# Where a scheduler puts scores, norms and key preparations in a top-k attention with two MoE layers, and which engine makes the low parts

## Chip, cores and metric

The kernel runs on one core of one Trainium2 chip. The metric is device time in microseconds, the median of several executions. The engines are TensorE (PE in the rows; PEld is its weight load), VectorE (DVE), ScalarE (ACT), GpSimd (POOL) and SyncE (SP), whose queue issues the DMAs. Each engine works through its instructions in order.

## The reference

For 4 batches, 8 heads, 576 positions and head dimension 64, attention keeps the 32 largest scores of each row, then two MoE layers follow on the 2304 x 512 result.

```python
scores = scale * np.matmul(q, k.transpose(0, 1, 3, 2))
kth = np.partition(scores, -top_k, axis=-1)[..., -top_k:-top_k + 1]
scores = np.where(scores >= kth, scores, -1000000000.0)
attn = np.exp(scores - np.max(scores, axis=-1, keepdims=True))
attn = attn / (np.sum(attn, axis=-1, keepdims=True) + 1e-09)
x = attn @ v                                        # -> (2304, 512)
x = ((1 / (1 + np.exp(-(x @ w_gate)))) * (x @ w_val)) @ w_out
h = np.maximum(x @ w_in, 0.0)
out = (h * h) @ w_out2
```

## The kernel before

**Chunks and blocks.** The 2304 rows are 18 row tiles of 128, and these form 11 chunks: tiles 0, 1, 2, 3 singly (chunks 0 to 3), then 4 and 5 (chunk 4), 6 and 7 (chunk 5), 8 and 9 (chunk 6) and so on to 16 and 17 (chunk 10). Attention works on pairs of heads of a chunk; a *block* is one row tile with one head, 144 in all, 8 in a small chunk and 16 in a large one. A name such as `S_11_0` in an order is tile 11, head 0; `x_6` belongs to chunk 6.

**A block.** `queries` (line 307) transposes a tile's queries on TensorE and splits them into a high part that ScalarE casts (L319) and a low part that DVE subtracts (L320). `scores` (L344) multiplies with the split keys into the one PSUM tile `sp`, and ScalarE copies the result to a tile `S` (L347; four buffers). `softmax` searches the 32 largest on DVE: four times `max` (L358) and three times `match_replace` (L364) into a working tile `W` (three buffers). Then GpSimd prepares thresholds (L372, L373, L380), ScalarE cuts and exponentiates (L376, L386, L387), GpSimd makes the low part of the weights inside `S` (L391, L394), and a transposing DMA on SP's queue (L410) brings them to `PT`. `values16` (L482) multiplies them with the values, ScalarE copies (L503) and GpSimd scales into the chunk's `xt` (L504).

**After a chunk.** `split_x` splits the finished x in two f16 parts: squares on ScalarE (L685), column norms with a matrix of ones on TensorE (L688), a reduce and a scale on DVE (L690), then the split itself. Then the chunk's MoE layers run, almost all of their time on TensorE (L738, L778, L841, L862).

**Keys and values.** `prep_keys` loads a batch's keys for a pair of heads, transposes them on TensorE, lets ScalarE cast the high part (L171) and DVE subtract the low part (L172), and stores both in DRAM, from which later blocks load them (`kst`, three buffers, L299). It is called one pair ahead of the first use. `prep_values` loads and squares values; `split_values` splits them and stores them (`vm` holds a buffer of `S`, `vom` one of `W`).

**What sets the order.** The attention is a generator, the MoE another; the main loop emits them interleaved, attention ahead of the MoE of the chunk before. A scheduler then orders each engine's instructions by its own model of time and by priorities. `add_manual_dep(..., NOSYNC)` is a dependence for this scheduler alone: it makes an instruction stand after another one in the scheduler's time and places no semaphore. In the generator, `head(n + 1)` emits the next block's scores, `tail` the values of an earlier block, and `late` is called by `softmax` when the searches are emitted:

```python
            with tc.high_priority(offset=int(up[0])):
                head(n + 1)
                if n > 0 and units[n - 1][0].ci < TCI:
                    tail(n - 1)
                if pr.ci >= TCI - 2:

                    def late(mark, n=n):
                        while late_values:
                            split_values(*late_values.pop(0), mark)
                        if units[n - 2][0].ci >= TCI:
                            tail(n - 2, mark)
```

## Time and profile before

| | before |
|---|---|
| median of 3 runs | 1325.46 us (1323.99 to 1329.02) |
| the profiled execution, its own time | 1327.31 us |
| span of its trace | 1325.5 us |
| mean granted clock of TensorE | 0.942 |
| busy: TensorE, DVE | 1190.7 us (90%), 999.0 us (75%) |
| busy: ScalarE, GpSimd | 807.8 us (61%), 809.7 us (61%) |
| largest groups on DVE | the searches, L358 and L364 |
| DMA | 157.95 MB, mean 119 GB/s |

The share of an engine is an average over stages that differ: the first 200 us convert weights, the middle runs searches next to MoE matmuls, the last 190 us are MoE alone. A matmul's end is modelled, so a busy TensorE is not TensorE at its peak. What a step is worth has to be read in its own stage.

### The profile page before, as it was taken

Reading aid. Unit: us, or ns where it says so; the run is one execution under the profiler, and the core shown is the slowest. Engines: PE = TensorE matmul, PEld = TensorE weight load, DVE = VectorE, ACT = ScalarE, POOL = GpSimd, SP = SyncE. Lnnn points to the kernel's source line nnn. Section 1 sums busy time; section 2 is a strip of 40 time slices with the busy share of each in tenths; the row PEclk is TensorE's granted clock in tenths of the full one; section 3 lists DMA queues with packets and bytes.
Section 4 is the critical chain, followed back from the end, with each engine's and each line's share of the span. In section 5 each row is a group of like instructions: output and inputs, shape, how many; then the busy total and the mean of one; then the engine's idle time right before and its main releaser. Section 6 shows DMA issues by size and latency. Waiting matters only on the chain.

```text
span 1325.5 us, 30239 instructions
## 1 busy us (share of the span) xinstructions
PE 1190.7 (90%) x11357; PEld 947.1 (71%) x11357; DVE 999.0 (75%) x2040; ACT 807.8 (61%) x1584; POOL 809.7 (61%) x1324
## 2 busy tenths in 40 slices
PE   6756999977989879889986999999999999999998
PEld 5544886865868758756874768877886887787775
DVE  6999996897899989887989777878999899210010
ACT  4777786776666676656666665656677657323122
POOL 1798868867566576557556764575657647424223
PEclk9658999979999979979996999999999999999999
DMA  7988851233356454656745255556444333100000
GB/s 196 330 285 293 269 178 28 77 100 101 102 120 144 115 129 98 147 115 155 179 109 128 72 128 136 123 124 152 100 100 108 97 82 65 44 1 1 17 1 16
DMA packets 263409, 157.95 MB, mean 119 GB/s; under 512 B 213344, under 2 KB 229728, under 8 KB 263264
## 3 DMA queue, kind: packets, MB, share of 16 engines
q1 hardware_dynamic: 263264, 156.03, 45.4%
q8 instruction: 89, 1.46, 0.5%
q14 instruction: 56, 0.46, 0.1%
HBM read 103.55 MB, written 19.40 MB: 93 GB/s over the span
## 4 chain that ended last, share of the span: by engine, by line
PE 54%; POOL 11%; DVE 10%; DMA 8%; ACT 8%; issue 6%; SPq 2%; ACTq 0%; POOLq 0%; DVEq 0%
PE ph L841 12%; PE acc L862 11%; PE pg L738 7%; PE pv L738 6%; PE acc L778 6%; PE sp L344 5%; DMA PT<-S 3%; DVE mx L358 3%; DVE W L364 3%; PE xp L482 3%; POOL S L391 2%; ACT W L387 1%; DMA kst<-ks 1%; ACT W L376 1%; ACT S L386 1%
## 5 line engine op out<-in xcount | busy, mean ns | idle before, releaser
L358 DVE MAX8 mx<-W 128x8 f32<-128x576 f32 x432 | 327.5, 758 | 10.5
L841 PE MATMUL ph<-x,wi_w 128*128 128x256 f16 (+1 forms) x1920 | 207.6, 262 | 7.1 <-ACT x L817 6.3
L364 DVE MATCH_REPLACE8 W<-mx,W 128x576 f32<-128x576 f32 x288 | 213.7, 742 | 0.0
L391 POOL TENSOR_TENSOR S<-W,S 128x512 f16<-128x512 f32 x112 | 130.0, 1160 | 128.7 <-ACT W L387 127.6
L862 PE MATMUL acc<-w_w,rh 128*128 128x512 f16 x816 | 194.8, 380 | 4.0 <-POOL rh L854 4.0
L841 PEld LDWEIGHTS <-wi_w 128*128 128x128 f16 x1920 | 167.9, 100 | 41.5 <-issue 9.9
L376 ACT ACTIVATE W<-S,bs 128x576 f32<-128x576 f32 x144 | 111.6, 775 | 106.7 <-POOL bs L372 106.2
L344 PE MATMUL sp<-kst,qt 128*128 128x288 f32 x608 | 139.2, 337 | 25.7 <-ACT S L347 14.5
L738 PE MATMUL pg<-xs,wg_w 128*128 128x256 f16 (+1 forms) x1440 | 157.7, 261 | 2.8 <-POOL xs L702 2.0
L738 PE MATMUL pv<-xs,wv_w 128*128 128x256 f16 (+1 forms) x1440 | 153.1, 258 | 1.2 <-ACT th L748 0.6
L738 PEld LDWEIGHTS <-wg_w 128*128 128x128 f16 x1440 | 124.6, 99 | 21.4 <-issue 3.7
L862 PEld LDWEIGHTS <-rh 128*128 128x128 f16 x816 | 77.1, 98 | 82.6 <-POOL rh L854 5.9
L347 ACT COPY S<-sp 128x576 f32<-128x576 f32 x144 | 91.6, 636 | 72.9 <-DMA PT<-S 36.3
L778 PEld LDWEIGHTS <-wo_w 128*128 128x128 f16 x1440 | 123.0, 99 | 17.9 <-issue 5.1
L738 PEld LDWEIGHTS <-wv_w 128*128 128x128 f16 x1440 | 123.1, 99 | 16.7 <-issue 3.4
L778 PE MATMUL acc<-gh,wo_w 128*128 128x256 f16 (+1 forms) x1200 | 123.4, 255 | 4.6 <-POOL gh L754 2.8
L344 PEld LDWEIGHTS sp<-kst,qt 128*128 128x128 f32 x608 | 93.6, 196 | 43.7 <-ACT S L347 20.0
L750 DVE TENSOR_TENSOR th<-pv,th 128x512 f32<-128x512 f32 (+1 forms) x60 | 36.2, 604 | 111.4 <-PE pv L738 105.1
L853 POOL TENSOR_TENSOR r<-r 128x512 f32<-128x512 f32 (+1 forms) x80 | 74.5, 932 | 72.7 <-ACT rh L852 66.3
L358 DVE MAX8 mx<-S 128x8 f32<-128x576 f32 x144 | 107.0, 743 | 9.4 <-ACT S L347 9.4
L364 DVE MATCH_REPLACE8 W<-mx,S 128x576 f32<-128x576 f32 x144 | 106.9, 742 | 0.0
L386 ACT ACTIVATE S<-W,bs 128x576 f16<-128x576 f32 x112 | 86.7, 775 | 19.5 <-POOL bs L380 15.7
(336 smaller groups left out, 2172.1 us busy)
## 6 DMA issues: line engine op xcount, KB each, us to landing
kst<-ks SPq DMA_DIRECT2D x104, 288.0 KB, 3.1
v<-vd SPq DMA_DIRECT2D x40, 320.0 KB, 3.2
qn<-in_q_dram SPq DMA_DIRECT2D x128, 64.0 KB, 2.3
wi_r<-in_moe_w_in_dram SPq DMA_DIRECT2D x16, 512.0 KB, 6.6
w_r<-in_moe_w_out_dram SPq DMA_DIRECT2D x16, 512.0 KB, 4.9
wg_r<-in_moe_w_gate_dram SPq DMA_DIRECT2D x12, 512.0 KB, 6.5
wv_r<-in_moe_w_val_dram SPq DMA_DIRECT2D x12, 512.0 KB, 6.9
wo_r<-in_moe_w_out_dram SPq DMA_DIRECT2D x12, 512.0 KB, 6.0
```

What stands on the lines that cost most here:

```text
L344: nc.tensor.matmul(sp[:, e, 0:HALF], l, r, start=(x == 0), stop=(x == len(ops) - 1))
L347: nc.scalar.copy(ss.rearrange("p (e s) -> p e s", e=2), sp[:, :, 0:HALF])
L358: m8 = nc.vector.max(mx[:, r], cur)
L364: nc.vector.match_replace(wk, mx[:, r], cur, NEG)
L376: nc.scalar.activation(wk, ss, AF.Prelu, bias=bs[:, 0:1], scale=1.0, alpha=BIG)
L386: nc.scalar.activation(pp[:, 0:S], wk, AF.Exp, bias=bs[:, 1:2], scale=SCALE)
L391: nc.gpsimd.tensor_tensor(pp[:, S + ST : 2 * S], wk[:, 0:SM], pp[:, 0:SM], op=ALU.subtract)
L738: nc.tensor.matmul(pp[:, e * N : (e + 1) * N], wblk(wd, a, c, f0, P), xs[:, b_, c, :], start=(e == 0 and n == 0), stop=(n == 3 * KM - 1), ...
L778: nc.tensor.matmul(acc[:, d // 2, (d % 2) * N : (d % 2 + 1) * N], wblk("wo", a, f, d * P, P), gh[:, b_, e * N : (e + 1) * N], start=(f == ...
L841: nc.tensor.matmul(ph[:, e * N : (e + 1) * N], wblk("wi", a, c, f0, P), x2[:, b_, c, :], start=(e == 0 and n == 0), stop=(n == 3 * KM - 1) ...
L853: nc.gpsimd.tensor_tensor(r, r, r, op=ALU.mult)
L862: nc.tensor.matmul(acc2[:, i, 0:DM], gh[:, b_, e * N + i * P : e * N + (i + 1) * P], wblk("w2", a, f, 0, DM), start=(f == 0 and x == 0), s ...
```

## The change

1. *Scores.* From chunk 4 on, `head(n + 1)` is called out of `late`, and each score matmul has an order dependence on the first `max` of the block before (`marks[0]`).
2. *Column norms of x.* From chunk 4 on, `square_x` lets ScalarE square x where x is finished; the norm matmuls come in the `late` of the next block, behind its last `max` (`marks[3]`).
3. *Late keys.* Batches 2 and 3 are prepared in the same pairs as the values of these batches, a chunk earlier than before. Loads go out at one block (`slots`), the rest (`finish_keys`) two blocks later behind the last `max`. The tail part of the keys lies in tag `we`, the high part in a buffer of `W` instead of `kst`. ScalarE copies the whole transposed keys over the loaded ones, and GpSimd subtracts instead of DVE. The values' tail part moves to tag `we` as well.
4. *Queries.* For all chunks: ScalarE copies the whole transposed queries over the loaded ones, and GpSimd subtracts the low part instead of DVE.

```diff
@@ prep_keys / finish_keys
+        tag, bufs = ("we", 3) if late else ("qn", 2)
+        ke = apool.tile([ST, 2, D], F32, tag=tag, bufs=bufs, name=f"ke_{b}_{hp}")
...
+        if late:
+            return kn, kv, ke
+        finish_keys(b, hp, kn, kv, ke, keep)
+
+    def finish_keys(b, hp, kn, kv, ke, keep=False, after=None):
+        tag, bufs = ("kst", KST) if after is None else ("W", 3)
+        kh = apool.tile([P, S], F32R, tag=tag, bufs=bufs, name=f"kp_{b}_{hp}")
...
+                if after is not None:
+                    tc.add_manual_dep(mm.ins, after.name, NOSYNC, reason="loaded by then")
...
+            else:
+                whole = kl.bitcast(F32)[:, c0 : c0 + w]
+                nc.scalar.copy(whole, pt[:, 0:w])
+                nc.gpsimd.tensor_tensor(
+                    kl[:, c0 : c0 + w], whole, kh[:, c0 : c0 + w], op=ALU.subtract
+                )
@@ queries
-                    nc.vector.tensor_tensor(
-                        qt[:, 1, :, sl], p3[:, :, sl], qt[:, 0, :, sl], op=ALU.subtract
+                    whole = qn.rearrange("p j a d -> p j (a d)")[:, :, sl]
+                    nc.scalar.copy(whole, p3[:, :, sl])
+                    nc.gpsimd.tensor_tensor(
+                        qt[:, 1, :, sl], whole, qt[:, 0, :, sl], op=ALU.subtract
                     )
@@ scores
+                    if after is not None:
+                        tc.add_manual_dep(mm.ins, after.name, NOSYNC, reason="free by then")
@@ attention
+            if n in slots:
+                late_k.append((*slots[n], *prep_keys(*slots[n], late=True)))
...
+                    if (b, pr.hp) not in done:
+                        done.add((b, pr.hp))
+                        slots[n + 1] = (b, pr.hp)
...
+                    elif after is not None:
+                        square_x(pr.ci, pr.xt)
+                        late_x.append(pr)
...
+                def late(marks, n=n, pr=pr):
+                    if pr.ci >= SCI:
+                        head(n + 1, marks[0])
+                        if units[n - 1][0].ci < TCI:
+                            tail(n - 1)
+                    todo_k = late_k[:]
+                    del late_k[:]
+                    while late_values:
+                        split_values(*late_values.pop(0), marks[3])
+                    while late_x:
+                        p = late_x.pop(0)
+                        xsp[p.ci] = split_x(p.ci, p.xt, marks[3])
+                    if units[n - 2][0].ci >= TCI:
+                        tail(n - 2, marks[3])
+                    for b, hp, kn, kv, ke in keys_due:
+                        finish_keys(b, hp, kn, kv, ke, after=marks[3])
+                    keys_due[:] = todo_k
```

How this moves instructions shows at three places. The first is TensorE's order where chunk 6 ends (`sp_11_0`, `sp_11_1`: scores of the next chunk's tile 11; `xp_9_3`: values of the last pair of chunk 6; `x_6pq`: its norms). Before:

```order
L344 MATMUL sp_11_0_10031<-kst_7_0_2_9543,qt_11_0_2_9730 128x288 x4
L344 MATMUL sp_11_1_10192<-kst_7_1_2_9753,qt_11_0_2_9730 128x288 x4
L482 LDWEIGHTS v_6_3_2_9264
L482 MATMUL xp_9_3_10046<-PT_9_6_9668,v_6_3_2_9264 64x128
...
L494 MATMUL xp_9_3_10046<-ident_81,z_9_3_9663 64x128 x2
L688 LDWEIGHTS ones_86
L688 MATMUL x_6pq_10083<-xs_6_10081,ones_86 128x256
...
L307 MATMUL qpt_10_1_10198<-ident_81,qn_10_1_9745 128x128 x2
```

And with the change:

```order
L364 MATMUL sp_11_0_10099<-kst_7_0_2_9604,qt_11_0_2_9792 128x288 x4
L506 LDWEIGHTS v_6_3_2_9323
L506 MATMUL xp_9_3_10105<-PT_9_6_9721,v_6_3_2_9323 64x128
...
L518 MATMUL xp_9_3_10105<-ident_81,z_9_3_9716 64x128 x2
L172 MATMUL kpt_3_0_0_10143<-ident_81,kn_3_0_9982 128x128 x3
L364 MATMUL sp_11_1_10264<-kst_7_1_2_9816,qt_11_0_2_9792 128x288 x4
L172 MATMUL kpt_3_0_4_10151<-ident_81,ke_3_0_9985 128x64
L324 MATMUL qpt_10_1_10270<-ident_81,qn_10_1_9808 128x128 x2
L713 LDWEIGHTS ones_86
L713 MATMUL x_6pq_10277<-xs_6_10140,ones_86 128x256
```

The second head's scores have moved from before the value matmuls to behind them; the norms have moved behind these scores and one tile's queries; a key preparation of batch 3 stands here that stood in the next chunk.

The second is DVE's order in the search of tile 7, head 7, the last block of chunk 5 (`kn_2_1`: keys of batch 2, second pair). Before:

```order
L364 MATCH_REPLACE W_7_7_8530<-mx_7_7_8531,S_7_7_8404 128x576
L818 SCALAR_TENSOR_TENSOR x2_4_8047<-acc1_4_7437,x2s_4_8059,x2_4_8047 128x512
L358 MAX mx_7_7_8531<-W_7_7_8530 128x8
L172 TENSOR_TENSOR kn_2_1_8487<-kpt_2_1_0_8493,kp_2_1_8492 128x512
L172 TENSOR_TENSOR kn_2_1_8487<-kpt_2_1_4_8500,kp_2_1_8492 128x64
L364 MATCH_REPLACE W_7_7_8530<-mx_7_7_8531,W_7_7_8530 128x576
L358 MAX mx_7_7_8531<-W_7_7_8530 128x8
```

And with the change:

```order
L388 MATCH_REPLACE W_7_7_8592<-mx_7_7_8593,S_7_7_8523 128x576
L381 MAX mx_7_7_8593<-W_7_7_8592 128x8
L388 MATCH_REPLACE W_7_7_8592<-mx_7_7_8593,W_7_7_8592 128x576
L381 MAX mx_7_7_8593<-W_7_7_8592 128x8
L388 MATCH_REPLACE W_7_7_8592<-mx_7_7_8593,W_7_7_8592 128x576
```

The search stands alone; the keys' subtractions have left DVE.

The third is GpSimd's order in the middle of chunk 5, between the low weight parts of tile 6, head 3 (`S_6_3`) and the thresholds of tile 7, head 2 (`bs_7_2`). Before:

```order
L391 TENSOR_TENSOR S_6_3_7181<-W_6_3_7231,S_6_3_7181 128x512
L394 TENSOR_TENSOR S_6_3_7181<-W_6_3_7231,S_6_3_7181 128x64
L401 TENSOR_SCALAR z_6_1_7202<-z_6_1_7202,vsc_88 128x2
L504 TENSOR_TENSOR xt_5_7131<-xr_7_0_7272 128x128
L372 TENSOR_SCALAR bs_7_2_7425<-mx_7_2_7417 128x1
```

And with the change:

```order
L415 TENSOR_TENSOR S_6_3_7251<-W_6_3_7285,S_6_3_7251 128x512
L418 TENSOR_TENSOR S_6_3_7251<-W_6_3_7285,S_6_3_7251 128x64
L425 TENSOR_SCALAR z_6_1_7263<-z_6_1_7263,vsc_88 128x2
L528 TENSOR_TENSOR xt_5_7187<-xr_7_0_7333 128x128
L189 TENSOR_TENSOR kn_2_1_7244<-kn_2_1_7244,kp_2_1_7336 128x512
L786 TENSOR_TENSOR gh_4_1_7480<-th_4_1_7476,gh_4_1_7480 128x512
L189 TENSOR_TENSOR kn_2_1_7244<-kn_2_1_7244,kp_2_1_7336 128x64
L340 TENSOR_TENSOR qt_6_2_1_7502<-qn_6_2_7151,qt_6_2_1_7502 128x256
L396 TENSOR_SCALAR bs_7_2_7506<-mx_7_2_7484 128x1
```

The keys' and a query tile's subtractions, and one MoE step, now stand in front of the thresholds.

## Rows read from the trace of the kernel before

**Rows 1.** The page: busy tenths and granted clock in 40 equal slices

```profile
DVE  6999996897899989887989777878999899210010
...
PEclk9658999979999979979996999999999999999999
```

**Rows 2.** Stretches: busy PE, PEld, DVE, ACT, POOL (instructions), clock, DMA share, GB/s

```profile
0.00:192.00 192.00, 140.15 (x960) 116.57 (x961) 176.62 (x331) 137.32 (x272) 132.25 (x139) 0.83 0.81 266
192.00:361.00 169.00, 148.20 (x1636) 122.37 (x1635) 138.72 (x271) 118.01 (x247) 123.79 (x191) 0.93 0.29 79
361.00:687.00 326.00, 294.38 (x3241) 236.27 (x3240) 286.06 (x612) 214.88 (x441) 202.60 (x405) 0.95 0.57 132
687.00:806.00 119.00, 101.94 (x891) 76.12 (x889) 95.48 (x208) 76.27 (x153) 79.05 (x144) 0.90 0.48 115
806.00:1134.00 328.00, 322.47 (x3167) 255.49 (x3165) 288.20 (x590) 213.12 (x394) 207.71 (x381) 0.99 0.47 105
1134.00:1325.00 191.00, 183.55 (x1475) 140.25 (x1473) 13.94 (x34) 48.17 (x78) 64.25 (x68) 0.99 0.04 12
```

**Rows 3.** Single lines: count, then duration in ns, minimum/median/maximum

```profile
L364 DVE MATCH_REPLACE8 W<-mx,W x288: 731/743/746, 13.9 to 1132.6; 128x576 f32<-128x576 f32 x144
...
L650 DVE SCALAR_TENSOR_TENSOR wi_w<-wi_c,wis,wi_w x7: 1273/1677/3319, 237.2 to 292.5; 128x1024 f16<-128x1024 f32 x7
```

**Rows 4.** DVE's groups, 0 to 192, then 192 to 361: busy, mean ns, idle before

```profile
L320 DVE TENSOR_TENSOR qt<-qpt,qt 128x256 fp32r<-128x256 f32 x9 | 3.7, 409 | 1.1 <-ACT qt L319 1.1
...
L320 DVE TENSOR_TENSOR qt<-qpt,qt 128x256 fp32r<-128x256 f32 (+1 forms) x9 | 3.4, 378 | 0.0
...
L418 DVE RECIPROCAL rz<-bs 128x1 f32<-128x1 f32 x16 | 2.4, 153 | 6.3 <-POOL bs L417 6.2
```

**Rows 5.** DVE's groups from 361 to 687 us

```profile
L320 DVE TENSOR_TENSOR qt<-qpt,qt 128x256 fp32r<-128x256 f32 (+1 forms) x28 | 10.8, 387 | 7.6 <-ACT qt L319 7.5
...
L172 DVE TENSOR_TENSOR kn<-kpt,kp 128x512 fp32r<-128x512 f32 (+1 forms) x8 | 3.5, 450 | 7.9 <-ACT kp L171 7.9
...
L690 DVE TENSOR_REDUCE x_4cm<-x_4pq 128x1 f32<-128x256 f32 x1 | 0.4, 425 | 0.8 <-PE x_4pq L688 0.8
L690 DVE TENSOR_REDUCE x_5cm<-x_5pq 128x1 f32<-128x256 f32 x1 | 0.4, 425 | 2.1 <-PE x_5pq L688 2.1
```

**Rows 6.** Waits from 361 to 687 us: total us, times, longest us

```profile
PE kpt L164 <- DMA kn<-in_k_dram: 6.1, 2, 4.6
...
DVE W L364 <- DMA vd<-vom: 3.8, 2, 2.3
...
DVE W L364 <- POOL S L394: 2.8, 2, 1.9
```

**Rows 7.** Groups by form, whole run: forms near the added ones

```profile
L391 POOL TENSOR_TENSOR S<-W,S 128x512 f16<-128x512 f32 x112 | 130.0, 1160 | 128.7 <-ACT W L387 127.6
L853 POOL TENSOR_TENSOR r<-r 128x256 f32<-128x256 f32 x24 | 16.2, 680 | 4.6 <-ACT rh L852 3.9 <-ACT vs L205 0.2
...
L503 ACT COPY xr<-xp 128x256 f32<-128x256 f32 x56 | 20.2, 360 | 9.4 <-PE xp L494 9.3
```

**Rows 8.** Timeline where chunk 6 ends: start us, duration us, instruction, idle before

```profile
686.17 0.75 DVE L358 MAX8 mx<-W 128x8 f32<-128x576 f32 x1
...
696.07 1.29 SPq L410 DMA_TRANSPOSE PT<-S  x1
...
698.95 1.65 PE L482 MATMUL xp<-PT,v 128*64 128x128 f16 x27 [2.59 <-DMA PT<-S]
...
708.22 1.01 PE L688 MATMUL x_6pq<-xs,ones 128*128 128x256 bf16 x4 [6.41 <-ACT xs L685]
```

**Rows 9.** Waits of the whole run: total us, times, longest us

```profile
ACT S L347 <- DMA PT<-S: 36.3, 29, 4.0
...
DVE mx L358 <- ACT S L347: 9.4, 11, 2.6
...
SPq L299 <- PE sp L344: 81.3, 38, 4.1
```

More of the change, by code (lines that the diff above doesn't have):

```diff
@@ L67 @@
 XRB = 1
+SCI = 4
 PB = 10
@@ L143, in tile_topk_attention__then__two_moe_layers, with prep_keys @@
     kloc = {}
-    def prep_keys(b, hp, keep=False):
+    def prep_keys(b, hp, keep=False, late=False):
         src = k[b, 2 * hp : 2 * hp + 2]
@@ L163, in prep_keys @@
                 kp = P if c < CB else ST
-                nc.tensor.transpose(
+                mm = nc.tensor.transpose(
                     pt[:, w : w + kp],
@@ L193, in prep_values @@
             nc.sync.dma_start(vm[:, j], src[j, 0:SM].rearrange("(p c) d -> p c d", c=CB))
-        ve = apool.tile([P, 2, D], F32, tag="qn", bufs=2, name=f"ve_{n}")
+        ve = apool.tile([P, 2, D], F32, tag="we", bufs=3, name=f"ve_{n}")
         for r in range(2):
@@ L319, in queries, with scores @@
                     nc.scalar.copy(qt[:, 0, :, sl], p3[:, :, sl])
-                    nc.vector.tensor_tensor(
-                        qt[:, 1, :, sl], p3[:, :, sl], qt[:, 0, :, sl], op=ALU.subtract
+                    whole = qn.rearrange("p j a d -> p j (a d)")[:, :, sl]
+                    nc.scalar.copy(whole, p3[:, :, sl])
+                    nc.gpsimd.tensor_tensor(
+                        qt[:, 1, :, sl], whole, qt[:, 0, :, sl], op=ALU.subtract
                     )
                     self.qt[(tt, b)] = qt
-        def scores(self, j, i):
+        def scores(self, j, i, after=None):
             tt = self.tts[i]
@@ L343, in scores @@
                 for x, (l, r) in enumerate(ops):
[L344 removed]
+                    mm = nc.tensor.matmul(
                         sp[:, e, 0:HALF], l, r, start=(x == 0), stop=(x == len(ops) - 1)
                     )
+                    if after is not None:
+                        tc.add_manual_dep(mm.ins, after.name, NOSYNC, reason="free by then")
             nc.scalar.copy(ss.rearrange("p (e s) -> p e s", e=2), sp[:, :, 0:HALF])
@@ L367, in softmax @@
             if late is not None:
-                late(m8.ins)
+                late(marks)
             bs = apool.tile([P, 4], F32, tag="bs", bufs=3, name=f"bs_{tt}_{h}")
@@ L680, in tile_topk_attention__then__two_moe_layers, with split_act @@
     SPLIT = ((0, 0), (0, 1), (1, 0))
-    def split_act(src, name, xs, N):
+    def split_act(src, name, xs, N, after=None):
         sq = xs[:, 1].bitcast(BF16)
-        nc.scalar.activation(sq, src, AF.Square)
+        if after is None:
+            nc.scalar.activation(sq, src, AF.Square)
         pq = ps_t.tile([P, 512], F32, tag="tr", name=name + "pq")
         for c in range(KM):
-            nc.tensor.matmul(pq[:, 0:N], ones, sq[:, c], start=(c == 0), stop=(c == KM - 1))
+            mm = nc.tensor.matmul(pq[:, 0:N], ones, sq[:, c], start=(c == 0), stop=(c == KM - 1))
+            if after is not None:
+                tc.add_manual_dep(mm.ins, after.name, NOSYNC, reason="squared by then")
         cm = mpool.tile([P, 1], F32, tag="xcm", bufs=2, name=name + "cm")
@@ L693, in split_act, with square_x, split_x @@
         return s, inv
-    def split_x(ci, xt):
+    def square_x(ci, xt):
+        N = len(chunks[ci]) * P
+        xs = xsl[ci] = mpool.tile([P, 2, KM, N], F16, tag="m4", bufs=M4, name=f"xs_{ci}")
+        nc.scalar.activation(xs[:, 1].bitcast(BF16), xt, AF.Square)
+    def split_x(ci, xt, after=None):
         N = len(chunks[ci]) * P
@@ L699, in split_x @@
             xs = mpool.tile([P, 2, KM, N], F16, tag="m4", bufs=M4, name=f"xs_{ci}")
-        sx, ix = split_act(xt, f"x_{ci}", xs, N)
+        sx, ix = split_act(xt, f"x_{ci}", xs, N, after)
         nc.gpsimd.tensor_scalar(xt, xt, sx, 1.0, op0=ALU.mult, op1=ALU.mult)
@@ L1014, in keys, with head @@
                         prep_keys(b, pairs[pi].hp, keep=pairs[pi].ci == 0)
-        def head(n):
+        late_x = []
+        late_k = []
+        slots = {}
+        keys_due = []
+        def head(n, after=None):
             if n >= len(units):
@@ L1044, in head @@
                 pairs[pi + 1].load_keys(0)
-            ready[n] = pr.scores(j, i)
+            ready[n] = pr.scores(j, i, after)
             if j == 1 and i == len(pr.tts) - 1 and pi + 1 < len(pairs):
@@ L1085, in attention @@
             late = None
-            with tc.high_priority(offset=int(up[0])):
-                head(n + 1)
-                if n > 0 and units[n - 1][0].ci < TCI:
-                    tail(n - 1)
-                if pr.ci >= TCI - 2:
-                    def late(mark, n=n):
-                        while late_values:
-                            split_values(*late_values.pop(0), mark)
-                        if units[n - 2][0].ci >= TCI:
-                            tail(n - 2, mark)
+            if pr.ci < SCI:
+                with tc.high_priority(offset=int(up[0])):
+                    head(n + 1)
+                    if n > 0 and units[n - 1][0].ci < TCI:
+                        tail(n - 1)
+            if pr.ci >= TCI - 2:
+                def late(marks, n=n, pr=pr):
+                    if pr.ci >= SCI:
+                        head(n + 1, marks[0])
+                        if units[n - 1][0].ci < TCI:
+                            tail(n - 1)
+                    todo_k = late_k[:]
[10 more added lines that the diff above has]
+                    keys_due[:] = todo_k
             work[n] = pr.softmax(j, i, ready.pop(n), late)
```

16 lines of the change are left out of this document (10 added, 6 removed).

## The prediction, made before the changed kernel was run

> **What bounds the kernel now.** I read the stages first. In the 40 slices of the page [rows 1] VectorE (DVE) is busy at 6 to 9 tenths in the first 34, which is where the searches are, and at 2 or less after; TensorE's granted clock falls to 5 to 8 tenths in seven of the first 22 and stays full after. The same by stretches [rows 2], cut where searches of a chunk begin or end: from 361 to 687 us DVE is busy 286.06 of 326 us and TensorE 294.38, at a mean clock of 0.95 of its upper level; from 687 to 806 TensorE drops to 101.94 of 119 at 0.90; from 806 on it is busy 322.47 of 328, and after the last search 183.55 of 191. So there are two regimes. Before some 730 us the attention sets the pace: its searches run one after another on DVE, and TensorE waits for the x of a chunk. After that TensorE has a backlog of MoE work and sets the end alone: the last search ends near 1134, 191 us before the end.
>
> The hand-over between the regimes can be followed at chunk 6 [rows 8]. Its last search ends at 686.92 (686.17 + 0.75). The transposing DMA of that block's weights is issued at 696.07, the value matmuls start at 698.95 after 2.59 us of waiting for it, and the norm matmuls of x_6 start at 708.22 after TensorE idled 6.41 us. From then on TensorE is dense. **What counts is therefore how early the search of chunk 6 ends**; DVE time saved after 687 us I count at nothing, because TensorE's backlog covers it (322.47 of 328 busy).
>
> **The change, part by part**, summed up to 687 us.
>
> *Low parts of queries.* The subtraction on DVE (L320) goes. Up to 687 us it is 9 + 9 + 28 instructions with 3.7 + 3.4 + 10.8 = 17.9 us busy, and DVE idled 1.1 + 0 + 7.6 = 8.7 us in front of them, for ScalarE's cast [rows 4, 5]. DVE is in order, so a search stood still meanwhile. Both go: 26.6 us. If the scores are late anyway the 8.7 us stay as another wait; that is the lower bound, 17.9.
>
> What replaces it: per tile a copy on ScalarE, 360 ns by the nearest row, the 128x256 copy out of PSUM, and a subtraction on GpSimd (POOL), 680 ns by the nearest 128x256 row [rows 7]. From 361 to 687 that is 28 x 0.36 = 10.1 us on an ACT that is idle 326 - 214.88 = 111 us, and 28 x 0.68 = 19.0 us on a POOL that is idle 123 us [rows 2]. Throughput costs nothing. Order in POOL's queue does: the thresholds of the next search stand behind these subtractions. In the stretch 192 to 361 DVE already waits 6.3 us over 16 reciprocals for POOL [rows 4]; 9 subtractions of 0.68 could add up to 6.1 us. I take half, 3 us; nothing is the lower end, as POOL idles between.
>
> *Late keys.* Eight preparations (batches 2 and 3) lose their two subtractions on DVE; four of them lie before 687: 3.5 us busy and 7.9 us of waiting in front [rows 5]. That wait is a transpose held up in TensorE's order by the key load, 6.1 us in two waits [rows 6]. The load now goes out two blocks before its transposes, so wait and work both go: 11.4 us. ACT gets two copies more and POOL two subtractions, at most 1.16 us each by the 128x512 row [rows 7]: 4 x 2.3 = 9.3 us of POOL's 123, covered. The seven DMAs of each (three loads, four stores) are the same as before but now stand in SP's queue among the value loads of the same pair; a transposing DMA behind them is issued later. I put that into the wait for scores below.
>
> The key's high half now holds a buffer of the searches' working tile W (three exist) until its store has landed. The value preparations do that today: four in this stretch, for which DVE waits 3.8 + 2.8 = 6.6 us [rows 6], 1.65 each. Four late keys: 6.6 us more. Ends: nothing, and 18.4, which is two waits for each key, as long as the longest here, 2.3.
>
> *Column norms.* The reduce stays, but it no longer stands in front of DVE's search waiting for TensorE: 0.8 + 2.1 = 2.9 us [rows 5]. The chain x to MoE becomes no shorter: the norms wait for the last maximum of a block, and in the order they have moved past three groups only.
>
> *Scores.* They cost the same matmuls, at a later place. Today they run well ahead, so DVE waits for a copied score only 9.4 us in 11 waits of the whole run [rows 9]. Behind the first maximum of the block before, about 4.7 us of that block's search (four maxima of 0.76, three replacements of 0.74 and their loads) are left for matmul, queueing and copy. In the order shown above, scores now also stand behind the value matmuls, which wait for a landing 12 us after a search's end [rows 8]. From 361 to 687 there are 48 searches. I take one in four waiting 0.85 us (9.4 / 11): 10.2 us. Ends: nothing; and each of the 24 second heads waiting 1.25 us (36.3 / 29, ACT's wait for the same transposes [rows 9]), 30 us.
>
> *A shared port.* POOL gets two-input work while DVE searches. The replacement of the search has kept 731 to 746 ns over 288 executions, with POOL busy 60% of the time; so it costs 0, while the weight splits, with two full inputs in SBUF, spread from 1273 to 3319 ns [rows 3]. The Trainium skill ("SBUF — State Buffer", Who interferes with whom) says that a DVE instruction with two SBUF inputs and a GpSimd instruction that reads SBUF share a port, and the second blocks entirely. Were the replacement such an instruction (it names the maxima and W), the rule would put up to 46 x 0.68 = 31 us on the searches; the trace of the replacement does not show it, that of the splits agrees.
>
> **Sum:** 26.6 + 11.4 + 2.9 = 40.9 saved; 3 + 6.6 + 10.2 = 19.8 given back; net 21 us by 687, and the end moves with it. The profiled execution took 1327.31 us (span 1325.5 and 1.8 around it), 1.85 above the median 1325.46. 1327.3 - 21 = 1306, so about **1304 us** as a median. Its own range, with costs between a third and one and a half times mine (6.6 to 29.7 us): 1291 to 1314.
>
> **The rivals.** *All of it arrives* (chance 0.17): no search waits for a score and W never runs short; 40.9 us come off, some 1284 us. For it: ACT and POOL have 111 and 123 us of idle time. Against it: both buffers and queues are waited for today.
>
> *Nothing arrives* (0.19): DVE's time turns into waits for W and for scores near their upper ends, 3 + 18 + 20 = 41 us, or the attention chain behind the search (12 us to the landing, then values, norms, split) was the limit and not DVE; also what happens if the dependences, which only order the scheduler and place no semaphore, leave the real order as it was. About 1325.
>
> *Scores behind value matmuls become the bound, and it is slower* (0.17). TensorE is in order; the second head's score stands behind value matmuls that wait for a transposing DMA, SP issues that DMA behind key loads which themselves wait for scores to free a key buffer, 81.3 us in 38 waits already [rows 9]. Then a late score delays a search, which delays the next landing. Price: the 2.59 us of the wait seen at 698.95 [rows 8] for each of 24 pairs, 62 us, against 40.9 - 9.6 = 31.3 saved: 31 us slower, 1356. It decides from 31.3 / 24 = 1.3 us a pair. For it: the landing at 12 us leaves no reserve. Against it: the landing is often earlier, DVE's wait for scores is 9.4 us today.
>
> **How the numbers follow.** The forecast has 0.47. Half a percent, 6.6 us, is what a measurement of this kernel tells from no change. Faster by more: 0.47 + 0.17 = 0.64; within: 0.19; slower: 0.17. The range reaches down past the full saving, to 1274, and up through the second rival and a third of the third, to 1338; some 0.07 lies below and 0.11 above.
>
> **What would show it.** No subtraction of queries on DVE in the trace, DVE's waits for ACT's cast gone, the search of chunk 6 ending 21 us earlier, near 666, and x_6 with it; TensorE above 95% from there; DVE's wait for the score copy near 10 us from 361 us up to there (9.4 in the whole run today), and waits for W near 13. It would be wrong if the search of chunk 6 ended early and the end did not follow (TensorE was not the bound after it), or if DVE's wait for score copies passed 31 us by then.

## The result, and the profile after

| | before | after |
|---|---|---|
| median | 1326.99 us (4 runs, 1323.99 to 1329.02) | 1340.02 us (4 runs, 1337.06 to 1341.46) |
| ratio | | 1.0097, 95% interval 1.0069 to 1.0125 |
| span of the profiled execution | 1325.5 us | 1339.7 us |
| mean granted clock | 0.942 | 0.936 |
| busy: TensorE, DVE | 1190.7, 999.0 us | 1203.7, 983.0 us |
| busy: ScalarE, GpSimd | 807.8, 809.7 us | 833.9, 874.2 us |

The change makes the kernel slower by 1%. DVE is busy 16.0 us less, and the end of the profiled execution comes 14.2 us later.

The page's slices of after, beside [rows 1]: the regimes are the same, and the searches fill 34 slices as before.

```profile
DVE  6999978786799978789987678888999789011010
...
PEclk9567999988999888989996999999999999999999
```

The same stretches as [rows 2], cut at the same events (start of the searches of chunks 2, 4, 7 and 8, the last search's end), after. Columns as there:

```profile
0.00:209.50 209.50, 155.37 (x1089) 127.16 (x1090) 187.62 (x328) 149.29 (x296) 150.16 (x155) 0.83 0.76 245
209.50:375.70 166.20, 137.60 (x1554) 114.79 (x1553) 132.28 (x262) 115.21 (x247) 121.69 (x193) 0.92 0.32 82
375.70:695.00 319.30, 293.41 (x3186) 237.32 (x3186) 277.05 (x567) 219.66 (x471) 224.03 (x439) 0.94 0.58 134
695.00:821.00 126.00, 107.08 (x931) 81.29 (x928) 93.41 (x197) 84.65 (x178) 91.33 (x162) 0.89 0.54 128
821.00:1137.50 316.50, 316.16 (x3063) 249.02 (x3061) 278.85 (x561) 215.11 (x411) 218.54 (x403) 0.99 0.44 101
1137.50:1339.00 201.50, 194.04 (x1549) 147.43 (x1547) 13.76 (x33) 49.99 (x80) 68.45 (x72) 0.99 0.04 12
```

The loss stands in the first row: chunks 0 and 1 take 209.5 us in place of 192. From 375.7 to 695 the kernel is faster than before (319.3 against 326). The last search ends 3.3 us later (1137.47 against 1134.14) and the end comes 14.2 us later: what the searches regain after 821 us, TensorE, busy 316.16 of 316.5 there, doesn't.

Three waits of the whole run, after, beside [rows 9] (columns: total us, times, longest):

```profile
DVE mx L381 <- ACT S L369: 52.8, 26, 5.1
...
ACT S L369 <- DMA PT<-S: 7.6, 7, 3.9
...
DVE W L388 <- POOL S L418: 7.6, 9, 2.7
```

DVE's wait for a copied score rose from 9.4 to 52.8 us. ScalarE waits less for the buffers that the transposing DMAs free (36.3 before, 7.6 now), which fits scores that start later.

The timeline where chunk 6 ends. Two lines of before that [rows 8] doesn't have, the end matmuls of the values and the first MoE matmul of the chunk:

```profile
701.11 0.70 PE L494 MATMUL xp<-ident,z 128*64 128x128 f32 x4 [0.51 <-DVE z L473]
...
712.70 0.37 PE L738 MATMUL pg<-xs,wg_w 128*128 128x256 f16 x1
```

And after (the last search ends at 693.37, 692.61 + 0.76):

```profile
692.61 0.76 DVE L381 MAX8 mx<-W 128x8 f32<-128x576 f32 x1
...
701.67 2.03 SPq L434 DMA_TRANSPOSE PT<-S  x1
...
706.06 1.33 PE L364 MATMUL sp<-kst,qt 128*128 128x288 f32 x4 [3.08 <-ACT S L369]
707.32 1.70 PE L506 MATMUL xp<-PT,v 128*64 128x128 f16 x28
...
711.93 0.69 PE L518 MATMUL xp<-ident,z 128*64 128x128 f32 x4 [2.51 <-DVE z L497]
...
718.34 1.01 PE L713 MATMUL x_6pq<-xs,ones 128*128 128x256 bf16 x4 [1.58 <-ACT xs L725]
...
725.13 0.37 PE L770 MATMUL pg<-xs,wg_w 128*128 128x256 f16 x1 [4.39 <-ACT xs L719]
```

The values (707.32) stand behind scores that wait 3.08 us for a buffer; the end matmuls of the values wait 2.51 us for a reciprocal that DVE does behind a search; and the first MoE matmul waits 4.39 us for ScalarE's part of the split. From the search's end to the first MoE matmul of chunk 6 it is 31.8 us; before it was 25.8 (686.92 to 712.70).

So the 14.2 us fall into four parts, each measured from event to event in the two traces. To the start of chunk 4's searches +14.7 (361.0 to 375.7); from there to the end of chunk 6's -8.2 (325.9 to 317.7); from there to chunk 6's first MoE matmul +6.0; from there to the end +1.8 (612.8 to 614.6). Rounding makes their sum 14.3.

### The profile page after: what moved, and what is told of

It reads as the page before. It is cut to its first block, busy times and chain, and to the rows that moved or that the text cites. A ratio compares the mean times of both kernels' runs of the same rounds, so it can differ in the third digit from the quotient of the medians.

```text
span 1339.7 us, 30517 instructions
## 1 busy us (share of the span) xinstructions
PE 1203.7 (90%) x11357; PEld 957.0 (71%) x11357; DVE 983.0 (73%) x1944; ACT 833.9 (62%) x1680; POOL 874.2 (65%) x1420
## 4 chain that ended last, share of the span: by engine, by line
PE 61%; DVE 11%; POOL 10%; ACT 6%; DMA 5%; issue 5%; SPq 2%; ACTq 0%; POOLq 0%; DVEq 0%
PE ph L873 12%; PE acc L894 11%; PE pg L770 9%; PE pv L770 8%; PE acc L810 8%; PE sp L364 5%; PE xp L506 4%; DVE mx L381 3%; DVE W L388 2%; POOL S L415 2%; DMA vm<-in_v_dram 1%; DMA wi_r<-in_moe_w_in_dram 1%; DVE wg_w L674 1%; DMA kn<-in_k_dram 1%; PE qpt L324 1%
## 5 line engine op out<-in xcount | busy, mean ns | idle before, releaser
L381 DVE MAX8 mx<-W 128x8 f32<-128x576 f32 x432 | 327.6, 758 | 10.9
L873 PE MATMUL ph<-x,wi_w 128*128 128x256 f16 (+1 forms) x1920 | 204.4, 260 | 12.3 <-ACT x L849 11.9
L364 PE MATMUL sp<-kst,qt 128*128 128x288 f32 x608 | 148.2, 349 | 14.4 <-ACT S L369 9.8
L381 DVE MAX8 mx<-S 128x8 f32<-128x576 f32 x144 | 107.4, 745 | 53.0 <-ACT S L369 52.8
L782 DVE TENSOR_TENSOR th<-pv,th 128x512 f32<-128x512 f32 (+1 forms) x60 | 36.3, 606 | 131.5 <-PE pv L770 126.7
L364 PEld LDWEIGHTS sp<-kst,qt 128*128 128x128 f32 x608 | 98.6, 203 | 31.5 <-ACT S L369 13.0
```

The source lines that it names most:

```text
L364: mm = nc.tensor.matmul(sp[:, e, 0:HALF], l, r, start=(x == 0), stop=(x == len(ops) - 1))
L381: m8 = nc.vector.max(mx[:, r], cur)
L873: nc.tensor.matmul(ph[:, e * N : (e + 1) * N], wblk("wi", a, c, f0, P), x2[:, b_, c, :], start=(e == 0 and n == 0), stop=(n == 3 * KM - 1) ...
```

## The experiments

All runs are in five rounds beside the kernel before, whose median in these comparisons lies between 1329.16 and 1330.68 us. Ratios are to it.

| run | median us | ratio (95% interval) |
|---|---|---|
| changed, early queries by DVE | 1330.33 | 1.0009 (0.9988 to 1.0030) |
| changed, keys not late | 1344.23 | 1.0103 (1.0082 to 1.0123) |
| changed, scores early | 1349.83 | 1.0162 (1.0135 to 1.0188) |
| before, with the queries' part | 1344.54 | 1.0104 (1.0084 to 1.0123) |
| early queries by DVE, GpSimd writes beside | 1336.92 | 1.0055 (1.0035 to 1.0075) |
| the same, GpSimd subtracts beside | 1347.11 | 1.0130 (1.0109 to 1.0152) |
| that order, subtraction narrow | 1342.51 | 1.0101 (1.0078 to 1.0125) |
| that order, copy narrow too | 1341.45 | 1.0095 (1.0072 to 1.0118) |
| early queries by DVE, norms as before | 1346.62 | 1.0130 (1.0108 to 1.0151) |
| early queries by DVE, `ve` as before | 1327.72 | 0.9983 (0.9967 to 0.9998) |
| that, all queries by DVE | 1327.63 | 0.9982 (0.9960 to 1.0005) |
| that, keys not late | 1332.34 | 1.0015 (1.0000 to 1.0030) |
| scores and norms alone | 1328.66 | 0.9989 (0.9971 to 1.0006) |
| norms alone | 1328.11 | 0.9983 (0.9966 to 1.0001) |
| `ve` as before, norms behind 2nd max | 1325.80 | 0.9968 (0.9954 to 0.9982) |
| that, all queries by DVE | 1328.37 | 0.9988 (0.9967 to 1.0008) |
| `ve` as before, norms behind 1st max | 1328.13 | 0.9993 (0.9976 to 1.0009) |

### Which part loses

**Early queries.** In chunks 0 to 3 DVE subtracts the low part of the queries again; all else as changed.

```diff
+                    if self.ci < TCI:
+                        nc.vector.tensor_tensor(
+                            qt[:, 1, :, sl], p3[:, :, sl], qt[:, 0, :, sl], op=ALU.subtract
+                        )
+                    else:
                         whole = qn.rearrange("p j a d -> p j (a d)")[:, :, sl]
```

> The changed kernel, but in chunks 0 to 3 DVE subtracts the low parts of the queries as before. In the changed kernel the search of chunk 4 begins at 375.7 us instead of 361.0, and the end is 14 us later; up to there only the queries' part of the change can act on searches. Theory A (the 18 early subtractions, 16.6 us on GpSimd at 926 ns each, stand in front of thresholds and reciprocals that DVE waits for): chunk 4's search begins within 4 us of 361, and the time is 1322 to 1331. Rival B (the loss comes from late keys, scores and buffers, and the early shift is made up later by TensorE's backlog): chunk 4 earlier or not, the time stays at 1336 to 1343.

1330.33 us: the whole loss is gone, so it comes with the queries of the first four chunks. Chunk 4's searches start at 366.2 us, 9.5 us sooner than in the changed kernel, though not within 4 us of 361 as theory A had it; what keeps the other 5.2 is asked below, with the tag of `ve`.

**Keys not late.** The three lines that fill `slots` go; keys are prepared where the kernel before has them.

```diff
-                    if (b, pr.hp) not in done:
-                        done.add((b, pr.hp))
-                        slots[n + 1] = (b, pr.hp)
```

> The changed kernel without late keys: keys of batches 2 and 3 are prepared as before, one pair ahead, with their subtraction on DVE. Theory K (their buffers of S and W and their place in GpSimd's queue slow chunks 5 and 7): DVE's waits for the score copy, 16.3 us from 376 to 695 and 20.7 from 695 to 821, fall by half or more and the time is 1325 to 1333. Theory A (the early stretch decides): DVE loses in chunks 6 and 8 what it gains in 5 and 7, and the time stays within 5 us of 1340.

1344.23, ratio 1.0103 beside 1.0097 of the changed kernel, with intervals that overlap: the late keys lose nothing here, as theory A has it.

**Scores early.**

```diff
-SCI = 4
+SCI = 1000
```

> The changed kernel, but scores are emitted as before and without the order dependence on the first maximum. Theory C (scores behind value matmuls are the bound, the third rival of the prediction): DVE's wait for the score copy falls from 52.8 to about 10 us and the time falls by 20 us or more, below 1320. Theory A: DVE's waits move to W and to other instructions, chunk 4 still begins near 375, and the time falls by less than 8 us, 1332 to 1342.

1349.83, above the ranges of both theories. Putting the scores later helps the changed kernel; the third rival falls.

**The queries' part alone**, on the kernel before:

```diff
-                    nc.vector.tensor_tensor(
-                        qt[:, 1, :, sl], p3[:, :, sl], qt[:, 0, :, sl], op=ALU.subtract
+                    whole = qn.rearrange("p j a d -> p j (a d)")[:, :, sl]
+                    nc.scalar.copy(whole, p3[:, :, sl])
+                    nc.gpsimd.tensor_tensor(
+                        qt[:, 1, :, sl], whole, qt[:, 0, :, sl], op=ALU.subtract
```

> The kernel before with the queries' part of the change alone (ScalarE copies, GpSimd subtracts, in all chunks). Theory A: chunk 4's search begins 10 to 15 us later than at 361 and the time is 1333 to 1342. Rival B: without score, norm and key changes the queries' part gains what was forecast for it, 15 to 25 us, and the time is 1300 to 1312.

1344.54, a little above theory A's range: by itself it loses as much as the whole change. Chunk 4's searches start at 372.4, 11.4 us later than before.

### By what means

Four ways were open: GpSimd's busy time, its port, its standing still for ScalarE's copy, and the order. The scheduler counts the added work and plans the first 361 us anew. In the next two runs DVE makes the part that is used, and GpSimd does something beside it.

```diff
+                        nc.scalar.copy(whole, p3[:, :, sl])
+                        for _ in range(3):
+                            nc.gpsimd.memset(whole, 0.0)
```

> As the run in which DVE subtracts the queries of chunks 0 to 3 (1330.33 us), but in these chunks ScalarE also copies the whole queries, as in the changed kernel, and GpSimd then writes zeros three times over the copy (3 x 0.31 = 0.94 us by its row 'MEMSET 128x256', against 0.93 us a subtraction in the changed kernel): it stands in the same queue, waits for the same copy, and reads nothing; nobody uses what it writes. Port theory (GpSimd's subtraction takes the port that DVE's weight conversions need): about 1330 us, DVE's weight work as short as there, search of chunk 4 starting near 366. Queue theory (GpSimd stands still for the copy, 19.9 us in 18 waits before 376 us, with thresholds and weight steps behind it): about 1340, search of chunk 4 near 375. Chain theory (scores wait for GpSimd's low part): about 1330, since DVE makes the part that is used.

```diff
+                        nc.scalar.copy(whole, p3[:, :, sl])
+                        nc.gpsimd.tensor_tensor(
+                            whole, whole, qt.bitcast(F32)[:, 0, :, sl], op=ALU.subtract
+                        )
```

> The same kernel, but GpSimd subtracts the cast from the copy, in place, as in the changed kernel, and nobody uses the result; the part that the scores use is DVE's. Port theory: about 1340 us, and DVE's weight conversions longer than in the run that only writes (128x512 ones above 0.8 us on the mean). Queue theory: 1340 as well, and the run that only writes the same. Chain theory: about 1330, as what the scores use comes from DVE.

1336.92 and 1347.11, neither at a time that the three theories gave, about 1330 or about 1340. In both runs DVE makes the part that the scores use, so the chain theory doesn't explain the loss. Reading costs more than writing, and at first sight that is the port. The rows put the difference elsewhere. The GpSimd groups, first the writing run, then the reading one, are equally long:

```profile
L345 POOL MEMSET qn<- 128x256 f32 x48 | 15.6, 324 | 14.4 <-ACT qn L343 11.6 <-issue 1.6
```

```profile
L344 POOL TENSOR_TENSOR qn<-qn,qt 128x256 f32<-128x256 f32 x16 | 15.4, 961 | 14.5 <-ACT qn L343 12.9 <-issue 1.6
```

and up to chunk 4 DVE is busy equally long, 318.19 and 318.93 us (third figure of the stretches). What differs is DVE's idle time, 52.0 and 62.8 us.

```profile
0.00:370.20 370.20, 296.50 (x2626) 243.76 (x2627) 318.19 (x600) 261.94 (x538) 280.06 (x379) 0.90 0.56 174
```

```profile
0.00:381.70 381.70, 299.31 (x2662) 247.12 (x2663) 318.93 (x608) 263.84 (x542) 274.45 (x347) 0.86 0.55 170
```

The Trainium skill ("SBUF — State Buffer", Who interferes with whom) says that a GpSimd instruction which reads SBUF shares a port with a DVE instruction of two SBUF inputs, and that one blocks the other. By that rule the reading run could have kept DVE busy up to 15.4 us longer than the writing one; it was 0.7 us. But the two runs have different orders, so this pair doesn't price the rule. In one held order, below, 8.6 us of such subtractions less go with 4.3 us less of DVE's work, which agrees with it in kind.

**The order kept, the work taken out.** So the order had to be held fixed. The program of the reading run was left as the scheduler wrote it, and only afterwards its 16 spare subtractions (then also the 16 copies) were cut to one element a row. All other instructions, their order and their waits are the same.

```diff
+    names = {i.name for i in SHRINK}
+    for func in nc.m.functions:
+        for block in func.blocks:
+            rows = list(block.instructions)
+            for n, i in enumerate(rows):
+                if i.name in names:
+                    rows[n] = narrow(i)
+            block.instructions = rows
     r = _run(nc, [arrays], core_ids=[0])
```

> The run in which GpSimd subtracts beside DVE in chunks 0 to 3 (1347.11 us), with every engine's order, every wait and every copy of ScalarE left as they are; only after the scheduler has fixed them, the 16 spare subtractions of GpSimd are made one element wide instead of 256, so that they cost next to nothing and read next to nothing. Time theory (GpSimd's 15.4 us of subtractions, by their length or by the port, cost the time): 1330 to 1335. Order theory (the scheduler, which counts the added work, plans the first 361 us in another order, and that order is the slow thing): 1345 or above.

> The same order again, and ScalarE's 16 copies are made two elements wide or less too (one): of the added work of the first four chunks only its places in the order and its waits are left. Time theory: 1328 to 1332, as without the added work. Order theory: 1345 or above. In between, the distance to the run before it is what ScalarE's copies cost in this order.

1342.51 and 1341.45, between the ranges of the two theories: 1.0101 and 1.0095 of before, against 1.0130 with the work and 1.0009 without it and its order. So 0.86% of before, some 11 us, comes with the order and the waits. The other 0.35%, some 5 us, comes with the work that was cut; the intervals overlap here, but the traces show where it goes. The first stretch with the narrow subtractions, beside that of the reading run above:

```profile
0.00:377.30 377.30, 295.92 (x2670) 244.84 (x2671) 314.66 (x608) 263.47 (x542) 266.16 (x347) 0.86 0.56 172
```

DVE's 608 instructions are the same and in the same order. It idles as long as with the work (62.6 and 62.8 us) and is busy 4.3 us less (314.66 against 318.93). The rows of its 128 weight conversions and splits add up to 128.0 us in place of 132.3, and to 128.5 in the last run. So GpSimd's subtractions do lengthen DVE's weight work beside them. That they do it by the port was not tested apart from their length.

The cut wasn't complete. A subtraction of one element still takes 451 ns of GpSimd (961 before the cut), and GpSimd still stands still for the copies, in the last run:

```profile
L345 POOL TENSOR_TENSOR qn<-qn,qt 128x1 f32<-128x1 f32 x16 | 7.2, 451 | 13.4 <-ACT qn L344 11.8 <-issue 1.6
```

Were the remaining 7.2 us of it worth as much as the 8.2 that were cut (5 us for both cuts), some 4 of the 11 us would be theirs. An order without these waits was not tried, so order and waits are not told apart.

The last run's first stretch, beside that of the kernel before:

```profile
0.00:376.80 376.80, 298.10 (x2670) 246.69 (x2671) 315.15 (x608) 260.67 (x542) 266.40 (x347) 0.89 0.55 172
```

```profile
0.00:361.00 361.00, 288.35 (x2593) 238.94 (x2594) 315.34 (x601) 255.33 (x519) 256.04 (x329) 0.88 0.57 178
```

DVE is busy as long (315.15, 315.34) and idles 61.7 us in place of 45.7. Not all of the 15.8 us by which the stretch is longer come with the spare steps: in the run with early queries by DVE, which has none of them, chunk 4 starts at 366.2 (busy 311.89, idle 54.3). The order and the waits account for the 10.6 us from there to 376.8, 7.3 of them idle.

The changed kernel has an order of its own, which was not held fixed; what it shows is this. The second half of chunk 1's searches took 43.8 us before (148.4 to 192.2) and 58.7 after (150.8 to 209.5). DVE's groups of weight conversion in that stretch, first before, then after:

```profile
L607 DVE SCALAR_TENSOR_TENSOR w_c<-w_r,w_c 128x512 uint32<-128x512 uint32 x16 | 10.9, 720 | 0.0
...
L606 DVE TENSOR_SCALAR w_c<-w_c 128x1024 uint32<-128x1024 uint32 x8 | 7.2, 895 | 0.8 <-ACT w_c L592 0.8
...
L418 DVE RECIPROCAL rz<-bs 128x1 f32<-128x1 f32 x4 | 0.6, 155 | 1.2 <-POOL bs L417 1.2
```

```profile
L631 DVE SCALAR_TENSOR_TENSOR w_c<-w_r,w_c 128x512 uint32<-128x512 uint32 x16 | 12.1, 795 | 0.0
...
L630 DVE TENSOR_SCALAR w_c<-w_c 128x1024 uint32<-128x1024 uint32 x8 | 7.0, 878 | 3.8 <-ACT w_c L616 3.7
L674 DVE SCALAR_TENSOR_TENSOR wg_w<-wg_c,wgs,wg_w 128x1024 f16<-128x1024 f32 x3 | 6.1, 2033 | 0.0
...
L631 DVE SCALAR_TENSOR_TENSOR wi_c<-wi_r,wi_c 128x512 uint32<-128x512 uint32 x2 | 1.6, 838 | 0.0
L674 DVE SCALAR_TENSOR_TENSOR wv_w<-wv_c,wvs,wv_w 128x1024 f16<-128x1024 f32 x1 | 1.3, 1273 | 0.0
...
L442 DVE RECIPROCAL rz<-bs 128x1 f32<-128x1 f32 x4 | 0.6, 154 | 3.9 <-POOL bs L441 3.8
```

Four weight splits and two conversions (6.1 + 1.6 + 1.3 = 9.0 us) now stand among these searches; DVE waits 3.0 us more for ScalarE's casts and 2.7 more for GpSimd. Work that has only moved here is no loss in itself; over the whole stretch up to chunk 4 DVE is busy 4.6 us longer and idles 10.1 us more (55.8 against 45.7). GpSimd's query subtractions, after, up to 376 us:

```profile
L340 POOL TENSOR_TENSOR qt<-qn,qt 128x256 fp32r<-128x256 f32 (+1 forms) x18 | 16.6, 926 | 19.9 <-ACT qn L339 10.9 <-DMA ke<-in_k_dram 8.8
```

They take 926 ns each where the later 28 take 673 (375.7 to 695), and GpSimd stands 19.9 us in front of them (10.9 for ScalarE's copy, 8.8 for a key load), while thresholds and weight steps queue behind.

### What the other parts give without it

**The norms put back**, with early queries by DVE:

```diff
-                    elif after is not None:
+                    elif False:
                         square_x(pr.ci, pr.xt)
```

> As the run in which DVE subtracts the queries of chunks 0 to 3 (1330.33 us), and the squares and column norms of x are emitted where x is finished, as in the kernel before, for all chunks. In that run the first MoE matmul of chunk 6 starts 5.7 us later than in the kernel before although its last search ends only 1.2 us later. Theory N (the place of the norms, behind a later search's last maximum, costs those 4.5 us, and they carry to the end): about 1326 us, first MoE matmul of chunk 6 near 714. Rival (TensorE gets there no earlier because scores and keys stand before it): 1330.

1346.62, the opposite of theory N: where scores and keys come late, the late norms are worth 1.2%. In this run DVE waits 7.3 us for the norms of x_4 and 6.9 for those of x_6, in the run that it starts from 1.6 and 1.2.

**`ve` in its old tag**, with early queries by DVE:

```diff
-        ve = apool.tile([P, 2, D], F32, tag="we", bufs=3, name=f"ve_{n}")
+        ve = apool.tile([P, 2, D], F32, tag="qn", bufs=2, name=f"ve_{n}")
```

> As the run in which DVE subtracts the queries of chunks 0 to 3 (1330.33 us), and the values' tail part lies in tag 'qn' as in the kernel before. There chunk 4's searches start 5.2 us later than before, although in chunks 0 to 3 only this tag differs. Theory T (the tail part holds one of the three 'we' buffers that the weights' transposes use in that stretch): chunk 4 starts near 361, about 1326 us. Rival (the order of the stretch differs for other reasons, or the 5 us do not reach the end): 1330, or within 2 us of it.

1327.72, and chunk 4's searches start at 362.8 in place of 366.2: theory T, for 3.4 of its 5.2 us. The times' intervals overlap, so that these 3.4 us reach the end is not shown.

From this run, three more: all queries by DVE, keys not late, and both.

```diff
-                    if self.ci < TCI:
+                    if True:
...
-                    if (b, pr.hp) not in done:
-                        done.add((b, pr.hp))
-                        slots[n + 1] = (b, pr.hp)
```

> As the run with the values' tail part as before (1327.72 us, ratio 0.9983), but DVE subtracts the queries of all chunks, as before the change: what is left of it is scores, norms and late keys. Theory Q (only the port and the queue of the first 361 us made the queries' part a loss; later, where no weights are converted, it saves DVE 16 us of subtractions): slower than that run by 5 to 10 us, some 1335. Rival (DVE's time is covered later in any case, by scores that come late): the same, 1326 to 1330.

> As the run with the values' tail part as before (1327.72 us), with the preparations of late keys where the kernel before has them. In the changed kernel leaving them out moved 1340.0 to 1344.2. Theory K (they save part of the 11.4 us that the prediction put on them): 1332 or above. Rival (their buffer of W and their stores cost what they save): 1326 to 1330.

> Scores and norms alone, on the kernel before: queries on DVE and late keys as before. If the two parts taken away in the two runs beside this one add up, this run is theirs together: 1327.7 plus both differences. By theories Q and K some 1340, slower than before; by their rivals 1326 to 1330.

1327.63, 1332.34 and 1328.66. The late queries give nothing. The groups of the run with them on GpSimd, then on DVE:

```profile
L386 DVE MAX8 mx<-S 128x8 f32<-128x576 f32 x144 | 107.3, 745 | 52.2 <-ACT S L374 51.9
...
L339 DVE TENSOR_TENSOR qt<-qpt,qt 128x256 fp32r<-128x256 f32 x16 | 6.5, 409 | 1.1 <-ACT qt L336 1.1
```

```profile
L386 DVE MAX8 mx<-S 128x8 f32<-128x576 f32 x144 | 107.1, 744 | 29.1 <-ACT S L374 28.8
...
L339 DVE TENSOR_TENSOR qt<-qpt,qt 128x256 fp32r<-128x256 f32 (+1 forms) x80 | 30.8, 386 | 22.2 <-ACT qt L336 21.9
```

With the late queries on GpSimd, 24.3 us of subtractions and 20.8 of waits in front of them leave DVE, and it waits 23.1 us more for scores. From chunk 4 to the last search it is busy 15.5 us less in all (648.9 against 664.4) and idles 14.4 more (113.3 against 98.9); the last search ends at 1125.1 and 1125.9. The late keys are worth 0.32% here, but not where they were put: without them chunk 6's search ends 1.5 us earlier (682.5 against 684.0), and from its first MoE matmul to the end it takes 621.2 us (1330.9 - 709.7) in place of 616.1 (1327.4 - 711.3). By the medians the keys' and queries' differences do not add up in the third run, but its interval overlaps that of the run without late keys.

**Norms sooner.**

```diff
-                        xsp[p.ci] = split_x(p.ci, p.xt, marks[3])
+                        xsp[p.ci] = split_x(p.ci, p.xt, marks[1])
```

> As the run with the values' tail part as before (1327.72 us), but the column norms stand behind the second of the four maxima of the search instead of behind the last, some 3 us sooner. Theory (the norms' place delays the MoE of a finished chunk, and the end follows it): 1325 us. Rival (TensorE then waits in order for squares that aren't there yet, with scores behind them, as where the norms were put back altogether, 1346.6): slower than 1330.

1325.80, the fastest here, 0.9968 (0.9954 to 0.9982) of before. Its interval and that of the run it starts from overlap.

Three that continue this: all queries by DVE (edit above), norms behind the first maximum, and norms alone (from the run with scores and norms alone).

```diff
-                        xsp[p.ci] = split_x(p.ci, p.xt, marks[1])
+                        xsp[p.ci] = split_x(p.ci, p.xt, marks[0])
...
-SCI = 4
+SCI = 1000
```

> As the run with the norms behind the second maximum (1325.80 us, ratio 0.9968), with the queries of all chunks on DVE. With the norms behind the last maximum this step changed nothing (1327.72 and 1327.63), though DVE is busy 15.6 us longer by it (992.4 against 976.8) and waits 23.1 us less for the score copy (28.8 against 51.9). Theory (where the subtraction leaves DVE after 361 us, a wait for scores takes its place): the same, 1324 to 1328. Rival (the norms' place was what hid the gain): slower, 1330 or above.

> As the run with the norms behind the second maximum (1325.80 us), with the norms behind the first of the four, one maximum and one replacement (1.5 us) sooner still. Theory (the sooner the norms, the sooner the MoE of the chunk, until TensorE waits for the squares): between 1324 and 1326. Rival (the squares are not there yet, TensorE waits in order, as where the norms were put back, 1346.6): above 1330.

> The norms' part alone on the kernel before: queries on DVE, late keys and scores as before, norms behind the last maximum. With scores and norms together it was 1328.66 (ratio 0.9989); with scores and keys but the norms put back 1346.62 against 1330.33. Theory P (the two belong together: the late scores lose time unless the norms move too, and early scores lose time if the norms move): slower than before by 5 us or more. Rival (each stands by itself, the norms gain their 16 us also alone): below 1320.

1328.37, 1328.13 and 1328.11: none better. The first is at the edge of what its theory gave (1324 to 1328), with an interval that overlaps that of the run it starts from; in the second and third neither theory holds. With early scores, moving the norms changes nothing that these runs can tell (0.9983, 0.9966 to 1.0001); with late scores and keys, putting them back cost 1.2%. All these variants, from the one with `ve` in its old tag on, lie within 0.35% of before.

## Why the prediction was wrong

*The regimes and the end* held. From the first MoE matmul of chunk 6 to the end it takes 612.8 us before and 614.6 after. What counts is when that chunk is ready, as said, but only to some 8 us: in the runs above the end takes 611.4 to 621.2, and 620.6 or more in the three in which GpSimd makes the late queries and the keys are prepared as before.

*Low parts of queries, up to 361 us* is the step that failed. It booked 3.7 + 1.1 + 3.4 saved and 3 for GpSimd's queue, a gain of 5.2; the stretch became 14.7 longer, 19.9 us off. The queries' part alone, on the kernel before, makes it 11.4 longer. Most of the rest is the tag of `ve`, 3.4 us with the early queries on DVE, for which the sum had no term at all. The sum priced instructions and a queue in the old order. But the scheduler plans this stretch by its own costs, weights and searches together, and two more steps a tile gave another plan. In the program whose order was held, the plan and its waits alone keep 0.86 of 1.21%. In the changed kernel itself, plan and work were not told apart. I had looked at the order in three places, none of them in this stretch, though a term of the sum lay there. Two more prices were low: 680 ns for a subtraction that took 926 there, and nothing for the 19.9 us that GpSimd stands in front of them.

*A shared port* was put at nothing for the searches, rightly: their replacements keep 743 ns at the median [rows 3], after:

```profile
L388 DVE MATCH_REPLACE8 W<-mx,W x288: 734/743/747, 14.3 to 1135.9; 128x576 f32<-128x576 f32 x144
```

For the weight splits the text had seen the spread and not priced it. After, the rows of the 128 weight conversions and splits add up to 138.2 us in place of 129.7, and DVE is busy 319.90 us up to chunk 4, 4.6 more than before, though the queries' rows (7.1 us) are gone. In the held order GpSimd's subtractions lengthened the same weight work by 4.3 us, so a term was missing here; how much of the 8.5 us in the changed kernel is theirs and how much the order's is not shown.

*From 361 us on* the forecast was -15.9 (18.4 + 11.4 + 2.9 saved, 6.6 + 10.2 given back), measured -8.2. The waits for ScalarE's casts and for the keys' load are gone. Two terms were too good. The first is the busy time: the sum took off the rows of the subtractions, 10.8 + 3.5 = 14.3 us, and DVE's busy time fell by 9.1 (286.06 to 277.01); these 5.2 us are most of the 7.7 that are missing. Rows can't be taken off whole, since each runs a little into the next: before, the maximum that starts at 686.17 ends at 686.92, and the next instruction starts at 686.84, so the rows of this stretch add up to some 306 us where DVE is busy 286. The second is the wait for scores, booked at 10.2; from 375.7 to 695 it is this, beside 0.6 before:

```profile
DVE mx L381 <- ACT S L369: 16.3, 10, 3.6
```

Against that, the 6.6 for the keys' buffer did not come: the waits for W went from 6.6 to 6.4. They had been misread, too. Only the 3.8 were the value preparations'; the 2.8 were waits for GpSimd's low weight parts, which read W [rows 6], and the 6.4 after are all of that kind. The lower bound of the queries' step, that its waits come back as a wait for scores, is what happened: up to that search's end DVE idles 0.8 us more than before.

*Column norms, the chain from x to MoE becomes no shorter*: it became 6.0 us longer, 1.9 up to the values, which stand behind a waiting score, 2.5 more up to their end matmuls, by the reciprocal behind a search, and 2.3 between the norms and the first MoE matmul; up to the norms 0.7 came back. No term stood for it.

*The rivals.* Scores behind value matmuls: such a place is in the timeline, but scores early are slower still, so it isn't the bound. Of Nothing arrives, the wait for scores was its right part. None of the rivals had a loss in the first 361 us, and neither of the two named signs of being wrong showed it: chunk 6's search ended late, not early, and DVE's wait for score copies up to there is 21.0 us (4.7 + 16.3), not past 31.

## What to carry to other kernels

Where a scheduler orders engines by its own model, an added instruction costs its time and the plan that comes with it. Read the order in each stretch in which a term of the sum lies, and to tell plan from work, keep the plan and take the work out. What taking an instruction away saves is not its row's time, where rows run into each other. Time taken off an engine that waits for its producer comes back as that wait; ask first what would be late next.

## What was not expected of the hardware

GpSimd's subtraction of 128x1 takes 451 ns, nearly half of the 961 for 128x256, so narrow instructions there are not cheap. Three writes of 128x256 (324 ns each) took as long as one subtraction. And in one held order, cutting GpSimd's 16 two-input subtractions from 15.4 to 6.8 us made DVE's weight conversions beside them 4.3 us shorter (132.3 to 128.0), with everything else in place.
